# Key tiles 4 to 15 from x stored by columns: means as a row, subtraction on GpSimd, 1/std behind the products

## The chip, the cores and the metric

One Trainium2 chip, one core. The metric is the device time of one execution in microseconds; 825.71 us is the median of three runs of the kernel before (825.45 to 825.81). The engines are PE (matrix products; PEld is its weight load), DVE (vector), ACT (scalar: functions with scale and bias), POOL (GpSimd) and SP, whose queue issues the DMAs. Each engine takes its instructions in order; they wait for each other through semaphores.

## The reference

2048 tokens of width 512 go through a layer norm without weights; a linear attention block (32 heads of 16) and a mixture of 8 experts with the best 2 taken per token both read the normed tokens, and both results are added to x:

```python
phi = lambda t: jnp.where(t > 0, t + 1, jnp.exp(t)) + 1e-6
pq, pk = phi(q), phi(k)
kv = jnp.einsum("bhsd,bhse->bhde", pk, v)
z = jnp.einsum("bhsd->bhd", pk)
num = jnp.einsum("bhqd,bhde->bhqe", pq, kv)
den = jnp.einsum("bhqd,bhd->bhq", pq, z)[..., None] + 1e-6
o = num / den
...
logits = xf @ w_gate
topk_idx = jnp.argsort(-logits, axis=-1)[:, :K]
...
xn = _layernorm(x, axis=-1)
return x + _A_ref(xn, A_wqkv, A_wo) + _B_ref(xn, B_w_gate, B_w1, B_w2)
```

## The kernel before, in words

The tokens lie in 16 tiles of 128 (`NT`). Products run in fp32r: each factor is split into a high part (a copy on ACT to fp32r, line 143) and a low part (DVE: the value less the high part, line 146), and three products (high-high, high-low, low-high: `PASSES`) stand for one.

The program opens with constants, a chain of small products that keep PE busy while the first loads arrive (`keep_warm`, line 214), and tiles 0 to 2 written out by hand. Then a loop runs over t = 3 to 15, and its code order is the order of every engine's queue. In step t:

- `k_proj(t)` (line 384): 24 products of the normed tile, transposed (`xnT`, high and low), with the key weights and the gate's: 12 of 256 columns and 12 of 264 (the last 8 are the gate's logits). The third product is the first that reads a low part.
- `transp_pe(t + 1)`: four transpositions on PE that put the next tile's normed tokens by columns into PSUM. Tiles from 5 on are first copied by DMA into an fp32r tile (`xr`, line 314) so that the transposition runs in fp32r (line 329); tiles up to 4 go in fp32 (line 331). `transp_split` takes xnT's high and low parts from PSUM.
- `k_feat(t)`: phi of the keys. ACT takes the exponential of each half (line 369), DVE the minimum with 1 and the added 1e-6 (line 371) and the maximum with 0 plus that (line 375, one operand in PSUM) and copies the logits out (line 404). GpSimd adds pk to z (`z_add`, line 411, on the tile `zz`).
- `xnhl` and `pkhl`: high and low parts of the normed tile and of pk.
- `g_acc(t - 1)` (line 437): 12 products of 512 columns that sum xn' pk of the tile before into four PSUM banks.
- Layer norm ahead of time, two tiles at once: DVE takes mean and variance (`ln_stat`, lines 273 and 274), GpSimd the power -0.5 (`ln_pow`, lines 280 and 281), DVE one Newton step in four small operations (`ln_fin`, lines 286 to 290), ACT the normed tile (`ln_out`, line 305), which DMA also stores in DRAM for the experts.
- In steps 5 to 10 one half of a weight matrix is split (`split_mat`, 1024 columns: wq0l to wo1l); in steps 12 to 14 DVE does the first of the routing (`piece`, lines 496 to 528).

PSUM holds four banks for the sums, two of tag `mm` for projections and two of tag `tr` for transpositions. `constants_b`, some 30 small GpSimd operations that the routing needs later, stands after step 2 in GpSimd's queue. After the loop come the first query projection (line 1386), the last `g_acc`, z, the product with the value weights, and then the queries and experts.

Of the kernel before, what the change touches and what calls it, by code (L numbers as in the profile page):

```python
# [86 lines left out]
def linear_attn_plus_moe(  # L87
# [8 lines left out]
    wkg: bass.AP,  # L96
    out: bass.AP,
# [7 lines left out]
    ps = ctx.enter_context(tc.tile_pool(name="ps", bufs=1, space=PSUM))  # L105
# [103 lines left out]
    L = cst.tile([P, NT, E], F32, name="L")  # L209

    def keep_warm(name, n, w=P):
        warm = psm("mm", name, w)
        for i in range(n):
            T.matmul(warm, ones_b, ones_b[:, :w], start=True, stop=True)

    def constants_a():
        V.memset(ones_b, 1.0)
        G.memset(eps_t, -0.5)
        idt = raw(um("idt"))[:, :P]
        make_identity(nc, idt)  # L220
        V.tensor_copy(ident_r, idt)
        keep_warm("warm", 102, 56)

    def constants_b():
# [4 lines left out]
        G.memset(eps6, 1e-6)  # L229
# [30 lines left out]
    xnT = [sm(f"xnT{t}").rearrange("p (h k c) -> p h k c", h=2, k=KC) for t in range(NT)]  # L260
# [6 lines left out]
    lnst = {}  # L267

    def ln_stat(g, i, t):
        if i == 0:  # L270
# [4 lines left out]

    def ln_pow(g, n):
        mv = lnst[g]
        sm = wp.tile([P, 4, 2], F32, tag="sm", name=f"sm{g}", bufs=4)
        va, r0, t0, nb = (sm[:, j, :n] for j in range(4))
        (V if g == 0 else G).tensor_scalar(va, mv[:, :n, 1], EPS, None, op0=ALU.add)  # L280
        G.tensor_tensor(r0, va, eps_t[:, :n], op=ALU.pow)
        lnst[g] = (mv, va, r0, t0, nb)

    def ln_fin(g, n):
        mv, va, r0, t0, nb = lnst[g]
        V.scalar_tensor_tensor(t0, r0, -0.5, r0, op0=ALU.mult, op1=ALU.mult)
        V.tensor_tensor(t0, t0, va, op=ALU.mult)
        V.scalar_tensor_tensor(r0, t0, 1.5, r0, op0=ALU.add, op1=ALU.mult)
        if g:
            V.scalar_tensor_tensor(nb, mv[:, :n, 0], -1.0, r0, op0=ALU.mult, op1=ALU.mult)  # L290

    def ln_fin_g(g, n):
        mv, va, r0, t0, nb = lnst[g]
# [4 lines left out]
        G.tensor_tensor(r0, r0, t0, op=ALU.mult)  # L298
        G.tensor_tensor(nb, nb, r0, op=ALU.mult)

    def ln_out(g, i, t, eng):
        mv, va, r0, t0, nb = lnst[g]
        xn[t] = ta(f"xn{t}")
        if eng is A:
            A.activation(xn[t], xt[t], AF.Identity, bias=nb[:, i:i + 1], scale=r0[:, i:i + 1])
        else:
            n = 1 if t else 2
            for c in range(n):
                o = slice(c * D // n, (c + 1) * D // n)
                V.tensor_scalar(xn[t][:, o], xt[t][:, o], mv[:, i, 0:1], r0[:, i:i + 1],  # L310
                                op0=ALU.subtract, op1=ALU.mult)
# [6 lines left out]
    xr = {}  # L318
# [5 lines left out]
    def transp_pe(t):  # L324
        xtp[t] = p = psm("tr", f"xtp{t}")
        for kc in range(KC):
            o = p[:, kc * P:(kc + 1) * P]
            if t in xr:
                T.transpose(o.bitcast(F32R), xr[t][:, kc * P:(kc + 1) * P], ident_r)
            else:  # L330
                T.transpose(o, xn[t][:, kc * P:(kc + 1) * P], ident)
# [31 lines left out]

    def phi(pq, srcs, name):
        e = ta(f"e_{name}")
        o = 0
# [4 lines left out]
        V.tensor_scalar(e, e, 1.0, 1e-6, op0=ALU.min, op1=ALU.add)
        o = 0
        for src in srcs:
            w = src.shape[-1]
# [26 lines left out]
    def k_feat(t, k1, k2):  # L401
        pk = ta(f"pk{t}")
        phi(pk, (k1, k2[:, :256]), f"k{t}")
        V.tensor_copy(L[:, t, :], k2[:, 256:264])  # L404
# [5 lines left out]
    def z_add(t):  # L410
        G.tensor_tensor(zacc, zacc if t > 1 else pks.pop(0), pks.pop(t), op=ALU.add)  # L411
# [6 lines left out]
    def two_lo(hl, src):
        split_lo(hl[:, 0], hl[:, 1], src)

    def two(name, src):
        hl = tb(name).rearrange("p (h c) -> p h c", h=2)
        split(hl[:, 0], hl[:, 1], src)
# [328 lines left out]
    pk = k_feat(0, k1, k2)  # L752
# [34 lines left out]
    ln_out(4, 1, 5, A)
    constants_b()
    load_x(8)
    load_x(9)  # L790

    for t in range(3, NT):
        ks = k_proj(t)
        if t < NT - 1:
# [13 lines left out]
        pkhl = two(f"pkhl{t}", pk)  # L808
# [583 lines left out]
    def q_exp(t):  # L1392
        qp = eq[t]
        e = ta(f"e_q{t}")
        A.activation(e, qp, AF.Relu, scale=-1.0)  # L1395
        A.activation(e, e, AF.Exp, scale=-1.0)
        A.activation(e, e, AF.Identity, bias=eps6)
# [397 lines left out]
```

## Time and profile before

| | |
|---|---|
| runs, median | 825.71 us |
| the profiled execution, its own time | 827.02 us |
| its span, first to last instruction | 825.3 us |
| granted PE clock | 1.000 |
| busy: PE, DVE, ACT, POOL | 99%, 82%, 65%, 30% |
| DMA, mean over the span | 155 GB/s |

The key loop lies between 24 and 102 us of the span. The view of stages, for six pieces of two steps each (columns: busy microseconds and instructions of PE, PEld, DVE, ACT and POOL, granted clock, DMA share, GB/s):

```profile
30.00:42.00 12.00, 12.00 (x82) 11.00 (x81) 8.56 (x24) 6.56 (x14) 4.34 (x5) 1.00 0.84 291
42.00:54.00 12.00, 12.00 (x82) 10.97 (x81) 10.62 (x25) 8.15 (x15) 4.62 (x5) 1.00 0.66 215
54.00:66.00 12.00, 12.00 (x82) 10.97 (x81) 10.62 (x25) 8.14 (x15) 4.62 (x5) 1.00 0.54 190
66.00:78.00 12.00, 12.00 (x82) 10.97 (x81) 10.61 (x25) 8.13 (x15) 4.61 (x5) 1.00 0.23 88
78.00:90.00 12.00, 12.00 (x82) 10.97 (x81) 9.65 (x28) 6.18 (x13) 4.09 (x5) 1.00 0.24 89
90.00:102.00 12.00, 12.00 (x79) 10.77 (x77) 10.90 (x39) 3.67 (x9) 1.86 (x2) 1.00 0.01 1
```

PE is busy throughout; DVE has about a tenth left in the middle pieces, POOL more than half.

How to read rows: a row of the timeline gives start, length, engine, line, operation, what it writes and reads, its shape, how many equal ones are merged, and in brackets the idle time before it and what ended it. A row of the groups gives busy time and the mean of one in ns. PE's products overlap, so their pace is read from their starts.

### The profile page before, as it was taken

The page shows a single profiled execution, that of the slowest core. Times are in us where ns is not written, and L with a number is a line of the kernel's source. Part 1 is how long each engine was busy: PE and PEld are TensorE (multiplying, and loading weights), DVE is VectorE, ACT ScalarE, POOL GpSimd, SP SyncE. Part 2 cuts the span into 40 slices and gives each one's busy share as a digit, 9 for nine tenths or more (in the row PEclk, how much of TensorE's full clock was granted, in tenths as well). Part 3 has the DMA queues.
Part 4 walks back from the last instruction along what each step waited for, and adds up shares of the span by engine and source line. Part 5 has one row for each costly group of instructions (what it writes and reads, how often), then busy time and mean ns, then how long its engine had stood idle before and what let it go on. Part 6 is the DMA issues. An engine that isn't in the chain of part 4 may idle for free. (4 is left out here: it accounts for less than half of the span.)

```text
span 825.3 us, 15895 instructions
## 1 busy us (share of the span) xinstructions
PE 819.3 (99%) x5361; PEld 748.5 (91%) x5361; DVE 679.8 (82%) x1469; ACT 540.2 (65%) x1155; POOL 250.7 (30%) x344
## 2 busy tenths in 40 slices
PE   9999999999999999999999999999999999999998
PEld 8999888888899999999999999999999998888886
DVE  7788889999989868877887888788888888887852
ACT  5575464358767666766776777677768777776750
POOL 5543234376310600042604340451227023311012
PEclk9999999999999999999999999999999999999999
DMA  4752136455865853474648465746566564549507
GB/s 167 237 204 98 52 122 209 132 179 195 242 204 149 174 167 108 144 174 145 136 140 225 121 130 157 202 108 163 160 179 140 152 176 108 111 134 231 149 3 176
DMA packets 106266, 127.96 MB, mean 155 GB/s; under 512 B 14718, under 2 KB 68734, under 8 KB 106150
## 3 DMA queue, kind: packets, MB, share of 16 engines
q1 hardware_dynamic: 92294, 106.69, 43.2%
q0 software_dynamic: 12880, 18.66, 11.9%
q10 hardware_dynamic: 1008, 1.57, 0.6%
q8 instruction: 43, 0.70, 0.4%
q14 instruction: 41, 0.34, 0.1%
HBM read 94.08 MB, written 31.22 MB: 152 GB/s over the span
## 5 line engine op out<-in xcount | busy, mean ns | idle before, releaser
L1183 POOL DMA_INDIRECT out_dram<-yo,sidx x22 | 35.1, 1595 | 278.8 <-DVE yo L1178 256.4
L1183 POOL DMA_INDIRECT out_dram<-yu,L x47 | 76.6, 1630 | 92.4 <-ACT yu L1276 60.8
L146 DVE TENSOR_TENSOR h<-hs,h 128x512 fp32r<-128x512 f32 (+7 forms) x112 | 78.5, 701 | 5.5 <-ACT h L143 5.1
L143 ACT ACTIVATE h<-hs 128x512 fp32r<-128x512 f32 (+7 forms) x112 | 72.3, 646 | 3.2
L1334 ACT ACTIVATE hs<-px 128x288 f32<-128x288 f32 (+7 forms) x54 | 21.1, 390 | 54.4 <-PE px L1326 52.7
L1349 ACT ACTIVATE hs<-hs 128x288 f32<-128x288 f32 (+7 forms) x54 | 23.0, 427 | 46.6 <-DVE hs L1348 44.9
L1353 DVE TENSOR_TENSOR hs<-px,hs 128x288 f32<-128x288 f32 (+7 forms) x54 | 23.4, 433 | 34.1 <-PE px L1326 33.3
L1348 DVE TENSOR_TENSOR hs<-pz,hs 128x288 f32<-128x288 f32 (+7 forms) x54 | 23.3, 431 | 32.7 <-PE pz L1326 30.3
L437 PE MATMUL gacc<-pkhl,xnhl 128*128 128x512 f32 x192 | 47.9, 397 | 0.0
L1050 POOL DMA_INDIRECT xg<-xn_d,gidx x37 | 41.1, 1111 | 20.3 <-issue 7.2
L437 PEld LDWEIGHTS gacc<-pkhl,xnhl 128*128 128x128 f32 x192 | 34.8, 188 | 6.8
L1182 POOL MEMSET spacer<- 1x1 f32 x69 | 37.8, 547 | 7.2 <-issue 7.2
L1354 ACT ACTIVATE hs<-hs 128x288 f32<-128x288 f32 (+7 forms) x54 | 22.8, 423 | 18.0 <-DVE hs L1353 16.2
L1359 DVE TENSOR_TENSOR hs<-py,hs 128x288 f32<-128x288 f32 (+7 forms) x54 | 23.0, 425 | 13.5 <-PE py L1326 12.8
L1426 POOL TENSOR_TENSOR pz<-pq,den 128x512 f32<-128x512 f32 x16 | 17.3, 1083 | 53.0 <-DVE den L1425 51.9
L411 POOL TENSOR_TENSOR zz<-zz,pk 128x512 f32<-128x512 f32 x14 | 18.2, 1296 | 48.2 <-DVE L L404 48.2
L1395 ACT ACTIVATE e_q<-qp 128x512 f32<-128x512 f32 x16 | 9.5, 597 | 35.3 <-PE qp L1386 31.6
L1207 PE MATMUL y<-w_5h,h 128*128 128x512 f32 (+2 forms) x88 | 32.0, 394 | 0.0
L1207 PE MATMUL y<-w_1h,h 128*128 128x512 f32 (+2 forms) x88 | 32.0, 393 | 0.0
L1207 PE MATMUL y<-w_2h,h 128*128 128x512 f32 (+2 forms) x88 | 32.0, 393 | 0.0
L1207 PE MATMUL y<-w_3h,h 128*128 128x512 f32 (+2 forms) x88 | 32.0, 393 | 0.0
L1207 PE MATMUL y<-w_4h,h 128*128 128x512 f32 (+2 forms) x88 | 31.7, 393 | 0.0
(676 smaller groups left out, 3161.3 us busy)
## 6 DMA issues: line engine op xcount, KB each, us to landing
wst<-in_B_w_dram SPq DMA_DIRECT2D x196, 128.0 KB
wst<-in_B_w_dram SPq DMA_DIRECT2D x36, 512.0 KB
zz<-in_B_w_dram SPq DMA_DIRECT2D x27, 512.0 KB
xs_d<-xg SPq DMA_DIRECT2D x119, 64.0 KB
xq<-xs_d SPq DMA_DIRECT2D x28, 256.0 KB
x<-in_A_x_dram SPq DMA_DIRECT2D x27, 256.0 KB
xn_d<-xn SPq DMA_DIRECT2D x16, 256.0 KB
xnT<-xn SPq DMA_DIRECT2D x11, 256.0 KB
```

Of the source, the lines that this page charges most:

```text
L143: A.activation(hi, src, AF.Copy)
L146: V.tensor_tensor(lo, src, raw(hi), op=ALU.subtract)
L437: T.matmul(gacc[d], xnhl[:, a, d * P:(d + 1) * P], pkhl[:, b, :], start=(t == 0 and i == 0), stop=(t == NT - 1 and i == 2))
L1050: G.indirect_dma_start(out=raw(t), out_offset=None, in_=xn_d, in_offset=IOA(ap=gidx[:, b:b + 1], axis=0))
L1182: G.memset(spacer, 0.0)
L1183: st = G.indirect_dma_start(out=rows, out_offset=IOA(ap=idx, axis=0), in_=src, in_offset=None, compute_op=ALU.add).ins
L1207: T.matmul(ya[r, d][:m], h[a][:, d * P:d * P + m], w[b][:, n % 2, :], start=(first and i == 0), stop=(last and i == 2))
L1348: V.tensor_tensor(c12, pz_, c12, op=ALU.add)
L1349: A.activation(c12, c12, AF.Silu)
L1353: V.tensor_tensor(c22, px, c22, op=ALU.add)
L1354: A.activation(c22, c22, AF.Silu)
L1359: V.tensor_tensor(c11, pz_, c11, op=ALU.add)
```

## The change

For tiles 4 to 15 the key projection no longer gets its transposed operand from PE. A second input, `xcols`, holds the same x by columns, two tiles in each row of blocks; SP loads 512 KB for a pair (`load_cols`). The means of a pair, one per token and so one per partition, are brought along the row: one transposition on PE for each tile of its column of means, repeated 128 times (`means_pe`), then a copy to half of `zz` (`means`, ACT). GpSimd subtracts them from the columns (`centre`), ACT and DVE split the result into xnT's parts (`cols_hi`, `cols_lo`). The factor 1/std is left out of xnT and comes in behind the products: as the scale of the exponential and Relu for keys, as a factor of the logits, and for the queries in `q_exp` and `q_norm` through `std`, `rneg` and `estd`.

With it, phi of the keys is written as min(Relu + 1, exp), with both halves in one ACT instruction from a PSUM tile of two banks, and the 1e-6 goes into pk's split and once into z; the copies to fp32r and the 44 fp32r transpositions go; x is loaded by pairs and earlier; PSUM is divided anew (`kk`: two tiles of two banks, which transpositions, rows of means and projections share; the query's pool opens when this one closes); the warm-up has 140 products of 39 columns for 102 of 56.

```diff
-    ps = ctx.enter_context(tc.tile_pool(name="ps", bufs=1, space=PSUM))
+    ps_a = ctx.enter_context(tc.tile_pool(name="ps_a", bufs=1, space=PSUM))
+    ps_k = ExitStack()
+    ps = [ps_k.enter_context(tc.tile_pool(name="ps_k", bufs=1, space=PSUM))]
...
+    def psk(name):
+        t = ps[0].tile([P, 2 * 512], F32, tag="kk", name=name, bufs=2)
+        return t.rearrange("p (a b) -> p a b", a=2)
...
+        G.memset(eps6, 1e-6)
...
-        keep_warm("warm", 102, 56)
+        keep_warm("warm", 140, 39)
...
-        G.memset(eps6, 1e-6)
...
+        G.memset(rneg[:, :TS], -1.0)
+        G.memset(std[:, :TS], 1.0)
+        G.memset(estd[:, :TS], 1e-6)
...
+    def scales():
+        V.reciprocal(std[:, TS:], rs[:, TS:])
+        G.tensor_scalar(rneg[:, TS:], rs[:, TS:], -1.0, None, op0=ALU.mult)
+        G.tensor_scalar(estd[:, TS:], std[:, TS:], 1e-6, None, op0=ALU.mult)
...
-        if t in COPIED:
-            xr[t] = xnT[t][:, 0].rearrange("p k c -> p (k c)")
-            Q.dma_start(raw(xr[t]), xn[t])
...
+    def load_cols(g):
+        xraw[g] = wp.tile([P, SW], F32, tag="s", name=f"xraw{g}", bufs=18)
+        Q.dma_start(xraw[g], xcols[g // 2])
...
+    def means_pe(g):
+        p = mrow[g] = psk(f"mrow{g}")[:, 0, :2 * P]
+        for i in range(2):
+            T.transpose(p[:, i * P:(i + 1) * P], lnst_mv[g][:, i, 0:1].broadcast_to([P, P]), ident)
+
+    def means(g):
+        A.activation(mslot(g), mrow.pop(g), AF.Copy)
+
+    def centre(t):
+        g, i = t & ~1, t % 2
+        src = xraw[g][:, i * D:(i + 1) * D]
+        xc[t] = ta(f"xc{t}") if t == NT - 1 else src
+        if i:
+            del xraw[g]
+        src, dst = (ap.rearrange("p (k c) -> p k c", k=KC) for ap in (src, xc[t]))
+        m = mslot(g).rearrange("p (i c) -> p i c", i=2)[:, i].unsqueeze(1).broadcast_to([P, KC, P])
+        G.tensor_tensor(dst, src, m, op=ALU.subtract)
...
+    def k_feat(t, k):
+        pk, r = ta(f"pk{t}"), ta(f"r{t}")
+        sc = rs[:, t:t + 1] if t >= TS else 1.0
+        for dst, fn in ((pk, AF.Exp), (r, AF.Relu)):
+            A.activation(dst.rearrange("p (a b) -> p a b", a=2), k[:, :, :256], fn, scale=sc)
+        V.scalar_tensor_tensor(pk, r, 1.0, pk, op0=ALU.add, op1=ALU.min)
+        if t >= TS:
+            V.tensor_scalar(L[:, t, :], k[:, 1, 256:264], sc, None, op0=ALU.mult)
...
+        if t == 6:
+            G.tensor_scalar(zacc, zacc, (NT - 1) * 1e-6, None, op0=ALU.add)
...
     for t in range(3, NT):
         ks = k_proj(t)
-        if t < NT - 1:
+        if t % 2 == 0 and t + 3 < NT:
+            means_pe(t + 2)
+        nxt = t + 1 if TS <= t + 1 < NT else None
+        if t + 1 < TS:
             transp_pe(t + 1)
-        xnhl = two(f"xnhl{t}", xn[t])
+        xnhl = two_hi(f"xnhl{t}", xn[t])
+        if nxt:
+            if t % 2:
+                centre(nxt)
+            cols_hi(nxt)
+        two_lo(xnhl, xn[t])
+        if nxt:
+            cols_lo(nxt)
         if t % 2 == 0 and t + 3 < NT:
             ln_fin(t + 2, 2)
+            if t + 4 == NT:
+                scales()
...
-        pk = k_feat(t, *ks)
+        pk = k_feat(t, ks)
+        if t % 2 == 0 and t + 3 < NT:
+            means(t + 2)
+        if nxt and t % 2 and nxt + 1 < NT:
+            centre(nxt + 1)
...
-        A.activation(e, qp, AF.Relu, scale=-1.0)
+        A.activation(e, qp, AF.Relu, scale=rneg[:, t:t + 1])
         A.activation(e, e, AF.Exp, scale=-1.0)
-        A.activation(e, e, AF.Identity, bias=eps6)
+        A.activation(e, e, AF.Identity, bias=estd[:, t:t + 1], scale=std[:, t:t + 1])
```

Three places show what stands in the queues. First GpSimd's queue behind `constants_b`, whose last instruction writes `lower`; before, z's sums (L411) and the next pair's power (L280, L281) follow it:

```order
L255 AFFINE_SELECT lower_113<-ones_r_97 128x64
L411 TENSOR_TENSOR zz_114<-zz_114,pk3_616 128x512
L280 TENSOR_SCALAR sm6_633<-mv6_535 128x2
L281 TENSOR_TENSOR sm6_633<-sm6_633,eps_t_98 128x2
L411 TENSOR_TENSOR zz_114<-zz_114,pk4_689 128x512
```

and now, with the subtractions (L384, on the columns `xraw`):

```order
L275 AFFINE_SELECT lower_115<-ones_r_100 128x64
L384 TENSOR_TENSOR xraw4_492<-xraw4_492,zz_116 128x512
L470 TENSOR_TENSOR zz_116<-zz_116,pk3_647 128x512
L384 TENSOR_TENSOR xraw4_492<-xraw4_492,zz_116 128x512
L301 TENSOR_SCALAR sm6_661<-mv6_566 128x2
L302 TENSOR_TENSOR sm6_661<-sm6_661,eps_t_101 128x2
L470 TENSOR_TENSOR zz_116<-zz_116,pk4_719 128x512
```

Tile 4's subtraction is the first thing behind the constants, and the power for tiles 6 and 7 stands behind tile 5's, which stands behind z's sum of pk(3).

Second, ACT's queue in step 9. Before, the exponentials of the two halves (L369) stand ahead of the next tile's xnT:

```order
L143 ACTIVATE xnhl9_1079<-xn9_866 128x512
L369 ACTIVATE e_k9_1083<-k1_9_1048 128x256
L369 ACTIVATE e_k9_1083<-k2_9_1049 128x256
L143 ACTIVATE xnT10_127<-xtp10_1074 128x512
L143 ACTIVATE pkhl9_1096<-pk9_1082 128x512
```

and now xnT of tile 10, from the subtracted columns, stands ahead of the exponential and Relu (L458):

```order
L150 ACTIVATE xnhl9_1079<-xn9_885 128x512
L150 ACTIVATE xnT10_1082<-xraw10_880 128x512
L458 ACTIVATE pk9_1086<-k_9_1054,rs_119 128x512
L458 ACTIVATE r9_1087<-k_9_1054,rs_119 128x512
L477 ACTIVATE pkhl9_1097<-pk9_1086,eps_t_101 128x512
```

Third, DVE's queue from the end of step 8 to pk's low part of step 9. Before:

```order
L146 TENSOR_TENSOR pkhl8_1021<-pk8_1002,pkhl8_1021 128x512
L146 TENSOR_TENSOR wv1l_1029<-wvst1_842,wv1h_1028 128x1024
L146 TENSOR_TENSOR xnhl9_1079<-xn9_866,xnhl9_1079 128x512
L371 TENSOR_SCALAR e_k9_1083<-e_k9_1083 128x512
L375 SCALAR_TENSOR_TENSOR pk9_1082<-k1_9_1048,e_k9_1083 128x256
L375 SCALAR_TENSOR_TENSOR pk9_1082<-k2_9_1049,e_k9_1083 128x256
L404 COPY L_116<-k2_9_1049 128x8
L146 TENSOR_TENSOR xnT10_127<-xtp10_1074,xnT10_127 128x512
L273 BN_STATS bs13_1093<-x13_888 128x6
L274 BN_AGGR mv12_1017<-bs13_1093 128x2
L146 TENSOR_TENSOR pkhl9_1096<-pk9_1082,pkhl9_1096 128x512
```

and now:

```order
L484 SCALAR_TENSOR_TENSOR pkhl8_1032<-pk8_1015,pkhl8_1032 128x512
L153 TENSOR_TENSOR wv1l_1039<-wvst1_862,wv1h_1038 128x1024
L153 TENSOR_TENSOR xnhl9_1079<-xn9_885,xnhl9_1079 128x512
L153 TENSOR_TENSOR xnT10_1082<-xraw10_880,xnT10_1082 128x512
L459 SCALAR_TENSOR_TENSOR pk9_1086<-r9_1087,pk9_1086 128x512
L461 TENSOR_SCALAR L_118<-k_9_1054,rs_119 128x8
L293 BN_STATS bs13_1094<-x12_822 128x6
L294 BN_AGGR mv12_1026<-bs13_1094 128x2
L484 SCALAR_TENSOR_TENSOR pkhl9_1097<-pk9_1086,pkhl9_1097 128x512
```

xnT's low part has moved ahead of pk and reads SBUF (`xraw`) for PSUM (`xtp`); pk is one operation of two SBUF tiles for three operations, two of which read PSUM (k1, k2).

More of the change, by code (lines that the diff above doesn't have):

```diff
@@ L209, in linear_attn_plus_moe @@
     L = cst.tile([P, NT, E], F32, name="L")
+    rs = cst.tile([P, NT], F32, name="rs")
+    rneg = cst.tile([P, NT], F32, name="rneg")
+    std = cst.tile([P, NT], F32, name="std")
+    estd = cst.tile([P, NT], F32, name="estd")
     def keep_warm(name, n, w=P):
-        warm = psm("mm", name, w)
+        warm = psk(name)[:, 0, :w]
         for i in range(n):
@@ L217, in constants_a @@
         V.memset(ones_b, 1.0)
-        G.memset(eps_t, -0.5)
+        G.memset(eps_t[:, :2], -0.5)
+        G.memset(eps6, 1e-6)
         idt = raw(um("idt"))[:, :P]
@@ L257, in constants_b @@
                         channel_multiplier=0)
-    xnT = [sm(f"xnT{t}").rearrange("p (h k c) -> p h k c", h=2, k=KC) for t in range(NT)]
+    xnT = {}
     def xT(t, hl, kc):
@@ L411, in z_add, with two_hi, two_lo, two @@
         G.tensor_tensor(zacc, zacc if t > 1 else pks.pop(0), pks.pop(t), op=ALU.add)
-    def two_hi(name, src):
+        if t == 6:
+            G.tensor_scalar(zacc, zacc, (NT - 1) * 1e-6, None, op0=ALU.add)
+    def two_hi(name, src, eps=False):
         hl = tb(name).rearrange("p (h c) -> p h c", h=2)
-        split_hi(hl[:, 0], src)
-        return hl
[L418 to L423, printed above, removed]
+        if eps:
+            A.activation(hl[:, 0], src, AF.Identity, bias=eps6)
+        else:
+            split_hi(hl[:, 0], src)
+        return hl
+    def two_lo(hl, src, eps=False):
+        if eps:
+            V.scalar_tensor_tensor(hl[:, 1], src, 1e-6, raw(hl[:, 0]), op0=ALU.add, op1=ALU.subtract)
+        else:
+            split_lo(hl[:, 0], hl[:, 1], src)
+    def two(name, src, eps=False):
+        hl = two_hi(name, src, eps)
+        two_lo(hl, src, eps)
         return hl
@@ L807, in linear_attn_plus_moe @@
             ln_stat((t + 4) & ~1, t % 2, t + 4)
-        pkhl = two(f"pkhl{t}", pk)
+            if t % 2 == 0:
+                load_cols(t + 4)
+        pkhl = two(f"pkhl{t}", pk, True)
         if t % 2 == 1 and t + 4 < NT:
@@ L818, in linear_attn_plus_moe @@
             piece(1 + (t == NE + 2))
-        if t % 2 == 0 and t + 7 < NT:
-            load_x(t + 6)
+        if t % 2 and t + 8 < NT - 1:
+            load_x2(t + 7)
+        elif t % 2 and t + 8 == NT - 1:
             load_x(t + 7)
+            load_x(t + 8)
+    ps_k.close()
+    ps[0] = ctx.enter_context(tc.tile_pool(name="ps_q", bufs=1, space=PSUM))
     M_v = []
@@ L1423, in q_norm @@
         den = dens.pop(t)
-        V.tensor_scalar(den, den, 1e-6, None, op0=ALU.add)
+        V.tensor_scalar(den, den, estd[:, t:t + 1], None, op0=ALU.add)
         V.reciprocal(den, den)
```

139 lines of the change are left out of this document (76 added, 63 removed).

## The prediction

> **What bounds the kernel now.** I read the page's first part, then the list of who waited for whom on PE, then PE's instructions in order of time.
>
> ```profile
> span 825.3 us, 15895 instructions
> PE 819.3 (99%) x5361; PEld 748.5 (91%) x5361; DVE 679.8 (82%) x1469; ACT 540.2 (65%) x1155; POOL 250.7 (30%) x344
> PE warm L214 <- DVE ones_b L217: 1.1, 1, 1.1
> ...
> PE xtp L331 <- ACT xn L305: 0.3, 1, 0.3
> 24.30 0.28 PE L384 MATMUL k<-wk1h,xnT 128*128 128x256 f32 x1
> 27.18 0.60 PE L331 MATMUL xtp<-ident_r,xn 128*128 128x128 f32 x4
> 27.54 3.00 PE L437 MATMUL gacc<-pkhl,xnhl 128*128 128x512 f32 x12
> 30.37 0.28 PE L384 MATMUL k<-wk1h,xnT 128*128 128x256 f32 x1
> 33.25 0.45 PE L329 MATMUL xtp<-ident_r,xnT 128*128 128x128 f32 x4
> 33.54 2.97 PE L437 MATMUL gacc<-pkhl,xnhl 128*128 128x512 f32 x12
> 36.35 0.28 PE L384 MATMUL k<-wk1h,xnT 128*128 128x256 f32 x1
> 96.42 0.28 PE L384 MATMUL k<-wk1h,xnT 128*128 128x256 f32 x1
> 102.29 0.50 PE L1386 MATMUL qp<-wq0h,xnT 128*128 128x512 f32 x1
> ```
>
> PE is busy in 99% of the span, and the four waits of its list (first and last shown) are short. So only PE's own row can be shortened, and whatever makes PE wait is paid in full. In the key loop the first column gives the pace: 24 projection products take 27.18 - 24.30 = 2.88 us, 12 products of the sum 30.37 - 27.54 = 2.83 us, four transpositions 33.54 - 33.25 = 0.29 us. One key tile lasts 36.35 - 30.37 = 5.98 us.
>
> **PE's own work.** Eleven tiles lose four transpositions at 0.29 us, tile 4 loses four of the fp32 kind at 27.54 - 27.18 = 0.36: 3.55 us gone. Six pairs get two single fp32 transpositions for the means, 0.36/4 = 0.09 each: 1.08 us (0.9 to 1.4, with 0.29/4 and a projection product's 0.12 as ends). Net **-2.5 us**. A key tile then takes 5.71 us on PE, 5.89 with a row of means: 11.6 us a pair.
>
> **The warm-up**, 102 products of 56 columns, becomes 140 of 39.
>
> ```profile
> 1.15 4.91 PE L214 MATMUL warm<-ones_b 128*128 128x56 bf16 x102 [1.15 <-DVE ones_b L217]
> 6.57 0.76 PE L359 MATMUL xtp<-ident_r,xn 128*128 128x128 f32 x4 [0.51 <-DVE xn L310]
> ```
>
> One starts every (4.91 - 0.23)/101 = 46 ns. If that is the price of an instruction, 140 end at 7.6 us and the first transposition, at 6.57 now, is 1.1 us late; if it is the columns' price, they end at 5.7 us and cost nothing. I take 0, since the total of columns is nearly the old one, and keep +1.1 for the range. The Trainium skill (TensorE: Matmul & The Clock Gate, "Wait — 56ns, not 53.3ns?") gives a start-to-start of N ÷ 1.2 GHz in a cold array, 46.7 ns for 56 columns; the measured 46 agrees, and by that rule the answer is 0.
>
> **A wait at tile 4.** Its columns need GpSimd's subtraction, and in POOL's queue that stands behind all of `constants_b`.
>
> ```profile
> 24.35 0.10 POOL L229 MEMSET eps<- 128x1 f32 x1
> 24.39 0.29 POOL L230 CAST ones_r<-ones_b 128x128 fp32r<-128x128 bf16 x1
> ...
> 28.94 0.30 POOL L255 TENSOR_SCALAR_AFFINE_SELECT lower<-ones_r 128x64 f32<-128x64 f32 x1
> 29.45 1.30 POOL L411 TENSOR_TENSOR zz<-zz,pk 128x512 f32<-128x512 f32 x1 [0.21 <-DVE L L404]
> L143 ACT ACTIVATE xnT<-xtp 128x512 fp32r<-128x512 f32 x15 | 8.9, 594 | 0.9 <-PE xtp L331 0.9
> L1426 POOL TENSOR_TENSOR pz<-pq,den 128x512 f32<-128x512 f32 x16 | 17.3, 1083 | 53.0 <-DVE den L1425 51.9
> ```
>
> The constants end at 28.94 + 0.30 = 29.24; one memset moves out, three small ones come (0.04 from start to start): about 29.4. The subtraction has no row; the nearest is GpSimd's sum of the same size, 1.30 (1.08 with the broadcast of L1426 is the other end). It ends at 30.7, ACT's high part (0.6) at 31.4, DVE's low part (0.68) at 32.1. PE would want tile 4 at 24.30 + 0.18 + 2.88 + 2.83 = 30.2, and its third product, the first with a low part, at 30.4. It gets it at 32.1: **+1.7 us** (+1.4 with 1.08). Behind the waiting `xnT4` on ACT stand the exponentials of tile 3, so all the evacuation that follows is late too.
>
> **The port between DVE and GpSimd.** This decides the rest.
>
> ```profile
> 30.77 0.66 DVE L146 TENSOR_TENSOR pkhl<-pk,pkhl 128x512 fp32r<-128x512 f32 x1
> 83.81 1.23 DVE L146 TENSOR_TENSOR pkhl<-pk,pkhl 128x512 fp32r<-128x512 f32 x1
> 83.19 1.30 POOL L411 TENSOR_TENSOR zz<-zz,pk 128x512 f32<-128x512 f32 x1 [2.85 <-DVE L L404]
> 187.69 2.39 DVE L146 TENSOR_TENSOR w_0l<-wst,w_0h 128x512 fp32r<-128x512 f32 x2
> 187.85 1.68 POOL L1407 TENSOR_TENSOR pz<-pq,zz 128x512 f32<-128x512 f32 x1 [0.55 <-DVE pq L1403]
> 53.07 0.68 DVE L146 TENSOR_TENSOR xnT<-xtp,xnT 128x512 fp32r<-128x512 f32 x1
> 53.22 1.30 POOL L411 TENSOR_TENSOR zz<-zz,pk 128x512 f32<-128x512 f32 x1 [4.77 <-DVE L L404]
> ```
>
> The low part of pk takes 0.66 us alone. Started under GpSimd's sum, it ends 0.55 after it (83.81 + 1.23 = 85.04 against 83.19 + 1.30 = 84.49): it stood still until GpSimd was through. At 187.69 two DVE instructions and one of GpSimd run strictly in turn: 0.55 + 1.29 + 0.55 = 2.39. The xnT row at 53.07, one operand from PSUM, is not slowed. Now the change moves work into this collision: xnT's low part reads xraw in SBUF instead of PSUM, pk comes from two SBUF tiles, and GpSimd gets a second large operation per tile. The Trainium skill (SBUF — State Buffer, "Who interferes with whom") says that a DVE instruction with two SBUF inputs contends with a GpSimd one that reads SBUF, and that the one issued later fully blocks. These rows agree; by that rule the new pk operation, which no row shows, waits as well, and the sum is the one below; were pk free, it would drop by little, since pk stands where GpSimd is idle.
>
> By the order of the queues a closed chain now runs from pk(t) to pk(t+1): GpSimd adds pk(t) to z, then subtracts a tile's means; ACT takes that tile's high part, and behind it in ACT's queue stand the exponential and Relu of t+1; DVE makes pk(t+1) from these. In between DVE's queue holds pk's, the weights', xnhl's and xnT's low parts, all with two SBUF inputs.
>
> ```profile
> 55.06 1.22 DVE L146 TENSOR_TENSOR wv0l<-wvst,wv0h 128x1024 fp32r<-128x1024 f32 x1
> 56.19 0.68 DVE L146 TENSOR_TENSOR xnhl<-xn,xnhl 128x512 fp32r<-128x512 f32 x1
> 55.30 1.54 POOL L281 TENSOR_TENSOR sm<-sm,eps_t 128x2 f32<-128x2 f32 x1
> 56.88 0.16 DVE L286 SCALAR_TENSOR_TENSOR sm<-sm 128x2 f32<-128x2 f32 x1
> 57.46 0.16 DVE L290 SCALAR_TENSOR_TENSOR sm<-mv,sm 128x2 f32<-128x2 f32 x1
> L1397 ACT ACTIVATE e_q<-e_q,eps 128x512 f32<-128x512 f32 x6 | 4.3, 724 | 0.2
> L1396 ACT ACTIVATE e_q<-e_q 128x512 f32<-128x512 f32 x6 | 3.8, 632 | 0.2
> L1395 ACT ACTIVATE e_q<-qp 128x512 f32<-128x512 f32 x6 | 3.6, 600 | 8.8 <-PE qp L1386 8.8
> 91.03 0.24 DVE L496 TENSOR_REDUCE arena<-arena 128x12 f32<-128x96 f32 x1
> 92.94 0.68 DVE L146 TENSOR_TENSOR xnhl<-xn,xnhl 128x512 fp32r<-128x512 f32 x1
> 97.03 0.16 DVE L516 TENSOR_SCALAR arena<-arena 128x12 f32<-128x12 f32 x1
> 100.75 0.69 DVE L146 TENSOR_TENSOR xnhl<-xn,xnhl 128x512 fp32r<-128x512 f32 x1
> ```
>
> - From an even tile, with a weight to split (8, 10): sum 1.35, pk low 0.55, subtraction 1.30, weight low 1.10 (start to start, 55.06 to 56.19), xnhl low 0.60, xnT low 0.60, pk 0.66: **6.15**. Tile 6 has a scaling of z on top (0.9; between 0.3 and 1.3): 7.1. Tile 4 has no weight; there ACT's path of 1.95 follows the subtraction: xnT high 0.65, exponential 0.60, Relu 0.70 (0.60 from PSUM by L1395; 0.1 more where the pipeline drains, for an operand from a tile, as L1397 against L1396): 3.2 + 1.95 + 0.66 = 5.8.
> - From an odd tile: GpSimd's power for the next pair now stands behind the subtraction, and DVE's four small Newton operations (56.88 to 57.62, 0.75) wait for it and stand ahead of pk: 5, 7, 9 take 3.2 + 1.1 + 0.2 + 0.55 + 0.6 + 0.75 + 0.66 = **7.05**; 3, without a weight, 6.6; 11, which also has no wait for the power left, 6.2.
> - A row of means takes one of the two projection buffers in PSUM, so product t + 1 waits for ACT's copy of it (0.4) behind Relu(t); in these sums that copy ends before pk(t) and adds nothing.
> - 12 and 13 have no weight but the routing's steps ahead of xnhl (92.94 - 91.03 = 1.9, part of it under GpSimd): 6.6 each.
>
> A pair with weights takes 13.2 us against PE's 11.6, so PE waits. Steps 3 to 13 add up to 6.6 + 5.8 + 7.05 + 7.1 + 7.05 + 6.15 + 7.05 + 6.15 + 6.2 + 6.6 + 6.6 = 72.4 us. pk(3) ends at 33.3 (xnT4 high begun at 30.75, then 0.6 for it, 0.6 and 0.7 for exponential and Relu, 0.66 for pk), so pk(14) at 105.7. Tile 15's third projection product, freed by the xnT low part just ahead of pk(14), comes at 105.1; it stands at 96.42 + 0.24 = 96.66 now: **+8.4 us**, in which PE's saving and tile 4's wait are contained.
>
> After that the first query product takes memory that tile 15's evacuation frees; behind pk(14) come 1.35 + 0.55, the routing's 100.75 - 97.03 = 3.7, xnhl 0.60, pk(15) 0.66 and the logits 0.15: 7.0, so 112.7 against 102.29: **+10.4 us**. From there on PE never waited for long and DVE, ACT and GpSimd do nearly the old work, so I pass it on whole; a scale or bias from a tile instead of a constant in the query features lies beside PE's rows. DMA changes from eleven copies of 256 KB to six loads of 512 KB, issued a pair ahead; I cost it at 0.
>
> 825.3 + 10.4 is a span of 835.7. The profiled execution itself took 827.02, 1.31 over the median 825.71 of the runs, so I take the same difference on the median: 836.0.
>
> **Rivals.** That the change doesn't do what it says is out: PE's order has no transposition of x behind tile 3.
> - *Half a chain.* If DVE's low parts slip between GpSimd's two operations better than I let them, only the port's own sum counts: 4 x 1.30 + 8 x 0.55 + 2 x 1.10 and 0.3 for small ones, 12.1 against 11.6 in three pairs: +1.5, with 1.7 and -2.5 some +0.7; anything up to +7 lies between. Against it: z's sum waits for pk(t), so GpSimd has nothing to do earlier. 827 to 833.
> - *Not slower.* The one mechanism is that the subtraction and the new DVE operations run side by side. Then the chain is 1.35 + 1.30 + 0.65 + 0.60 + 0.70 + 0.70 = 5.3 from an even tile and 1.35 + 1.30 + 0.45 + 1.3 + 0.75 + 0.70 = 5.9 from an odd one, 11.2 a pair: under PE's 11.6, the point from which it decides. What is left is -2.5 + 1.7 and some 0.5 behind tile 4: **825.4**. For it: no row has these very operations; against it: every 128x512 pair that met did block.
> - *Faster.* The same, and tile 4 is not late: 825.7 - 2.5 = 823.2. It needs the constants to end 1.7 us sooner; POOL's rows speak against it.
> - *Warm-up by the instruction*: +1.1 on any of them, 837.1.
>
> **How the numbers follow.** Forecast with its warm-up variant 0.66, half a chain 0.14, not slower 0.10, faster 0.08, beyond it all 0.02. The forecast's own range is 833 (subtraction at 1.08: 11 x 0.22 less, scaling 0.3) to 838.5 (warm-up, scaling 1.3, weight at 1.22). With the half chain this holds 0.8, so the range is 826.5 to 838.5. About 0.2% can be told from no change here: slower 0.79, within 0.13, faster 0.08.
>
> **What would show it.** PE waiting for xnT about 1.7 us at the fourth key tile and about 0.7 to 1 us in most later ones; DVE's low parts in the key loop at 1.2 or more in their means; GpSimd's subtraction at 1.3 or longer; the first query product at about 112. I am wrong if DVE's rows stay at 0.68 beside a busy GpSimd, if the subtraction of tile 4 starts before 29, or if PE shows no wait behind tile 5.

## The result, and the profile after

| | before | after |
|---|---|---|
| runs, median | 825.76 us (825.45 to 826.36, 4 runs) | 837.65 us (836.11 to 838.53, 4 runs) |
| ratio of the runs, 95% interval | | 1.0141 [1.0124, 1.0159] |
| span of the profiled execution | 825.3 us | 835.6 us |
| first query product begins | 102.29 us | 111.02 us |

The change costs 1.4%. The page of the changed kernel, first part, and then its list of who waited for whom on PE (microseconds in all, times, the longest):

```profile
span 835.6 us, 15855 instructions
PE 822.1 (98%) x5363; PEld 746.1 (89%) x5363; DVE 687.5 (82%) x1440; ACT 553.7 (66%) x1161; POOL 277.0 (33%) x362
```

```profile
PE k L427 <- DVE xnT L153: 2.7, 6, 0.8
PE qp L1478 <- DVE L L461: 2.1, 1, 2.1
PE k L427 <- ACT xnT L150: 1.8, 2, 0.9
...
PE k L427 <- ACT zz L374: 1.1, 3, 0.5
```

PE's busy time rose by 2.8 us although it has less to do, and three new waits stand where before there was none: for xnT's two parts, for the copy of the rows of means, and one of 2.1 us ahead of the first query product. PE's instructions of the changed kernel in order of time show where the 10.3 us of span arise:

```profile
30.79 0.38 PE L427 MATMUL k<-wk1h,xnT 128*128 128x256 f32 x1 [0.89 <-ACT xnT L150]
...
31.52 0.51 PE L427 MATMUL k<-wk1h,xnT 128*128 128x256 f32 x2 [0.22 <-DVE xnT L153]
...
103.27 0.51 PE L427 MATMUL k<-wk1h,xnT 128*128 128x256 f32 x2 [0.62 <-DVE xnT L153]
...
111.02 0.47 PE L1478 MATMUL qp<-wq0h,xnT 128*128 128x512 f32 x1 [2.09 <-DVE L L461]
...
118.20 0.39 PE L1478 MATMUL qp<-wq0h,xnT 128*128 128x512 f32 x1
```

Tile 15's third product is 103.27 - 96.66 = 6.6 us late, the first query product 111.02 - 102.29 = 8.7. The second query projection begins at 118.20, where it began at 107.86 before: 10.3. So 6.6 us come from the key loop, 2.1 from the wait behind it, and 1.6 from something between the first and the second query projection. The waits of PE's list in the loop come to only 5.6 us, and PE should have saved some there. PE's weight loads (PEld) tell the rest: between 20 and 125 us they wait 3.9 and 2.6 us for xnT's two parts, 3.2 for the copies of the rows of means and 1.8 for pk's low part, 11.5 us in all, where the kernel before has none of these. For the 1.6 us, the view of stages from 109 to 118 us (columns as in the table of six pieces) says what happens:

```profile
109.00:112.00 3.00, 0.98 (x4) 0.86 (x5) 2.27 (x7) 0.73 (x1) 1.12 (x1) 1.00 0.00 0
112.00:115.00 3.00, 3.00 (x9) 2.38 (x8) 2.66 (x12) 0.00 (x0) 0.63 (x2) 0.57 0.51 190
115.00:118.00 3.00, 3.00 (x13) 2.38 (x12) 0.67 (x5) 2.57 (x5) 0.00 (x0) 0.86 0.67 250
```

Behind the wait PE's granted clock, the number behind POOL's column, falls to 0.57 and 0.86: PE is busy throughout, but at little over half its pace, and 0.43 x 3 + 0.14 x 3 = 1.7 us are lost.

The port: GpSimd's and DVE's instructions of the changed kernel in order of time.

```profile
28.52 0.29 POOL L275 TENSOR_SCALAR_AFFINE_SELECT lower<-ones_r 128x64 f32<-128x64 f32 x1
28.80 1.28 POOL L384 TENSOR_TENSOR xraw<-xraw,zz 128x512 f32<-128x512 f32 x1
...
33.76 1.74 POOL L384 TENSOR_TENSOR xraw<-xraw,zz 128x512 f32<-128x512 f32 x1
...
52.75 1.83 POOL L472 TENSOR_SCALAR zz<-zz 128x512 f32<-128x512 f32 x1
```

```profile
31.74 0.69 DVE L459 SCALAR_TENSOR_TENSOR pk<-r,pk 128x512 f32<-128x512 f32 x1 [0.28 <-ACT r L458]
...
34.28 1.77 DVE L153 TENSOR_TENSOR xnhl<-xn,xnhl 128x512 fp32r<-128x512 f32 x1
...
46.42 2.31 DVE L153 TENSOR_TENSOR wq0l<-wqst,wq0h 128x1024 fp32r<-128x1024 f32 x1
...
103.13 0.68 DVE L459 SCALAR_TENSOR_TENSOR pk<-r,pk 128x512 f32<-128x512 f32 x1
...
110.05 0.68 DVE L459 SCALAR_TENSOR_TENSOR pk<-r,pk 128x512 f32<-128x512 f32 x1
```

The subtraction takes 1.28 us where DVE is idle (28.80) and 1.74 beside DVE's low parts; xnhl's low part, 0.68 alone, takes 1.77 beside it and ends 0.55 behind it (36.05 against 35.50); a weight's, 1.22 before, takes up to 2.31. The new pk operation runs where GpSimd is idle and keeps 0.69; the rows shown are those of tiles 3, 14 and 15.

### The profile page after: what moved, and what is told of

Read it like the earlier page. It is cut to its first block, busy times and chain, and to the rows that moved or that the text cites. A ratio compares the mean times of both kernels' runs of the same rounds, so it can differ in the third digit from the quotient of the medians.

```text
span 835.6 us, 15855 instructions
## 1 busy us (share of the span) xinstructions
PE 822.1 (98%) x5363; PEld 746.1 (89%) x5363; DVE 687.5 (82%) x1440; ACT 553.7 (66%) x1161; POOL 277.0 (33%) x362
## 5 line engine op out<-in xcount | busy, mean ns | idle before, releaser
L150 ACT ACTIVATE h<-hs 128x512 fp32r<-128x512 f32 (+7 forms) x112 | 72.4, 646 | 3.2
L1426 ACT ACTIVATE hs<-px 128x288 f32<-128x288 f32 (+7 forms) x54 | 21.1, 391 | 56.7 <-PE px L1418 56.6
L1487 ACT ACTIVATE e_q<-qp,rneg 128x512 f32<-128x512 f32 x16 | 11.0, 688 | 36.0 <-PE qp L1478 29.2
L1436 ACT ACTIVATE hs<-px 128x288 f32<-128x288 f32 (+7 forms) x54 | 21.2, 392 | 16.4 <-PE px L1418 15.1
```

The lines of the kernel that those rows point to most:

```text
L150: A.activation(hi, src, AF.Copy)
```

## The experiments

The theory: DVE's operations with two operands in SBUF stand still while GpSimd's new subtraction reads SBUF; by the order of the queues a closed chain from pk(t) over GpSimd and ACT to pk(t+1) sets the pace. Rivals: the port alone without the chain; DVE simply too full; GpSimd's queue, whatever it reads; the shared PSUM buffers. Ratios are to the kernel before on the same chip, with their 95% intervals.

**1. The chain cut.** All work stays; the sum for z comes one step later, so that no subtraction stands behind a sum that needs the newest pk.

```diff
-        if t > 2:
-            z_add(t)
+        if t > 3:
+            z_add(t - 1)
...
+    z_add(NT - 1)
     ps_k.close()
```

> GpSimd adds pk to z one step later, so that no subtraction stands behind a sum that waits for the newest pk. All work stays. Theory (closed chain through GpSimd's queue, on top of the shared port): the wait of the subtraction for pk(t) goes, what is left is the port's own sum, about 12.1 us a pair against 12.76 measured between pk(8) and pk(10); some 0.6 us in five to six pairs, 834 us (832 to 836). Rival A (the port alone: DVE loses the same time wherever GpSimd's two operations stand): within 1 us of 837.65. Rival B (only the queue's chain, the port is nothing): the first query product at 103 to 104, 828 us or less.

Measured: 837.76 us (836.9 to 839.15), 1.0144 [1.0127, 1.0161], the first query product at 111.85. Rival A held. Was the chain really cut? The list of ACT's waits between 30 and 112 us, of the changed kernel and then of this one:

```profile
ACT xnT L150 <- POOL xraw L384: 13.6, 9, 2.9
```

```profile
ACT xnT L150 <- POOL xraw L384: 4.0, 2, 2.9
```

It was: ACT's nine waits for GpSimd's subtraction became two. What DVE then did instead is in the groups of DVE's instructions in the loop (count | busy us, mean ns), again of the changed kernel and then of this one:

```profile
L484 DVE SCALAR_TENSOR_TENSOR pkhl<-pk,pkhl 128x512 fp32r<-128x512 f32 x11 | 12.1, 1104 | 1.3 <-ACT pkhl L477 1.3
L153 DVE TENSOR_TENSOR xnhl<-xn,xnhl 128x512 fp32r<-128x512 f32 x11 | 11.6, 1055 | 0.2 <-ACT xnhl L150 0.2
L153 DVE TENSOR_TENSOR xnT<-xraw,xnT 128x512 fp32r<-128x512 f32 x11 | 7.5, 686 | 3.4 <-ACT xnT L150 3.1
```

```profile
L153 DVE TENSOR_TENSOR xnhl<-xn,xnhl 128x512 fp32r<-128x512 f32 x10 | 11.9, 1191 | 0.4 <-ACT xnhl L150 0.4
L153 DVE TENSOR_TENSOR xnT<-xraw,xnT 128x512 fp32r<-128x512 f32 x11 | 11.2, 1017 | 2.8 <-ACT xnT L150 2.8
L484 DVE SCALAR_TENSOR_TENSOR pkhl<-pk,pkhl 128x512 fp32r<-128x512 f32 x11 | 9.7, 885 | 1.4 <-ACT pkhl L477 1.4
```

Against 0.66 to 0.68 alone these three stand still for 11 x 0.44 + 11 x 0.38 = 9.0 us in the changed kernel, and for 10 x 0.51 + 11 x 0.34 + 11 x 0.22 = 11.3 here. The weights' low parts gain (4.0 us of standstill become 0.9), small operations lose; with all of DVE's rows from pk(3) to pk(14), each one's time less what it takes alone, it is 14.7 us in the changed kernel and 16.4 here, and about 1.8 in as many steps of the kernel before. The subtraction, no longer held back, only meets other operations of DVE, and the steps from pk(3) to pk(14) take 71.6 us (33.08 to 104.64) where they took 71.4. So the chain is not what costs: without it the standstill is no less. One thing blurs this: PE's clock fell at tile 4 in this execution (see the last section), and DVE waited 0.70 us for Relu there, so up to 0.7 us of gain may be hidden.

**2. The subtraction on DVE**, at the same places in the program.

```diff
-        G.tensor_tensor(dst, src, m, op=ALU.subtract)
+        V.tensor_tensor(dst, src, m, op=ALU.subtract)
```

> The subtraction runs on DVE at the same places in the program. DVE gets 12 more operations of about 0.6 us from start to start (1.2 us a pair), GpSimd keeps the sum for z. Theory (chain and port): of 12.76 us a pair about 1.7 of blocking and 0.6 of waiting go, so the pair comes to 11.7 to 11.9, near PE's own 11.6; the wait for GpSimd's constants at tile 4 goes too. 829 us (827 to 831.5), xnhl's and the weights' low parts back at 0.68 and 1.22 except under the sum for z. Rival (DVE is simply full, each operation more costs): 12 x 0.6 = 7 us on top, 840 or more.

Measured: 832.22 us (831.0 to 832.29), 1.0067 [1.005, 1.0083]; the first query product at 105.00, 6.0 us sooner. DVE got twelve operations more and the kernel became 0.7% faster (the ratio was 1.0141), so DVE is not simply full. Two things go at once here: pk(3) starts at 29.30 where it started at 31.74, since nothing at tile 4 waits for GpSimd's constants any more, and that is 2.4 of the 6.0 us; the other 3.6 arise between pk(3) and pk(15). The groups of DVE:

```profile
L484 DVE SCALAR_TENSOR_TENSOR pkhl<-pk,pkhl 128x512 fp32r<-128x512 f32 x12 | 13.0, 1080 | 1.4 <-ACT pkhl L477 1.3
...
L153 DVE TENSOR_TENSOR xnhl<-xn,xnhl 128x512 fp32r<-128x512 f32 x11 | 7.5, 681 | 0.0
```

xnhl is back at 0.68; pkhl still meets the sum for z. The time is 0.7 us above the range expected: the wait ahead of the first query product stayed at 2.1 us, and the clock fell behind it here too (0.55 in 106 to 109 us).

**3. Without the subtraction** for tiles 4 to 14.

```diff
-        G.tensor_tensor(dst, src, m, op=ALU.subtract)
+        if t == NT - 1:
+            G.tensor_tensor(dst, src, m, op=ALU.subtract)
```

> Leaves out the subtraction of the means for tiles 4 to 14 (tile 15 keeps it); rows of means and their copies stay. Theory: without GpSimd's second operation neither chain nor most of the blocking is left, PE goes at its own pace and shows its saving of 2.5 us but for a first-query wait of 1 to 2 us: 825 us (823 to 828). Rival (the two shared PSUM buffers of the projections, or ACT's order, hold PE up, not the subtraction): 833 or more.

Measured: 826.03 us (825.06 to 827.5), 0.9998 [0.9988, 1.0008]; PE busy without a gap from 30 to 90 us, first query product at 100.26 behind a wait of 1.7. The subtraction, with its late start, is the whole cost: the PSUM buffers and ACT's order hold nothing up. And even at no price for it the change as written is no gain, since the wait behind the loop stays.

**4. The port alone**: the kernel before, with one more GpSimd operation for each key tile.

```diff
         if t > 2:
             z_add(t)
+            G.tensor_tensor(zb, xn[t], xn[t], op=ALU.subtract)
```

> The kernel before, with one more GpSimd operation for each key tile from 3 on, behind the sum for z: xn less xn, 128x512, into the unused half of zz. Nobody waits for its result. Theory (port): DVE's low parts of xnhl and of the weights wait for it, 0.5 to 1.2 us each; DVE has 1.4 us free in 12, so a pair of tiles comes to 12.3 to 13 us instead of 12: 829 us (827 to 832), and DVE rows of 1.2 us and more that were 0.68. Rival (GpSimd's work beside DVE costs nothing unless something waits for it): 825.8 within 0.8.

Measured: 831.4 us (830.93 to 831.87), 1.0062 [1.0045, 1.0079]. Nobody reads the result, and it costs 5 us. GpSimd's rows and then DVE's:

```profile
54.72 1.55 POOL L408 TENSOR_TENSOR zz<-xn 128x512 f32<-128x512 f32 x1
```

```profile
55.29 2.06 DVE L146 TENSOR_TENSOR wv0l<-wvst,wv0h 128x1024 fp32r<-128x1024 f32 x1
```

The weight's low part, 1.22 without it, ends 1.08 behind the dummy (57.35 against 56.27): nearly its whole length comes after the dummy's end.

**5. GpSimd busy without reading**: the same place, but an iota (it only writes); one for each tile (without the loop of the diff), and then three, since one took 0.56 us and left the length open.

```diff
         if t > 2:
             z_add(t)
+            for _ in range(3):
+                G.iota(zb, pattern=[[1, D]], base=0, channel_multiplier=0,
+                       allow_small_or_imprecise_dtypes=True)
```

> The kernel before, with one more GpSimd operation for each key tile from 3 on at the same place as the dummy subtraction, but one that reads nothing: an iota of 512 columns into the unused half of zz, estimated at about 1.1 us from the iota of 128 columns at 0.35 and of 64 at 0.23. Theory (DVE stands still only beside a GpSimd operation that reads SBUF): DVE's low parts keep their times, 826 (825.2 to 827). Rival (any GpSimd operation beside DVE holds it up, or the longer GpSimd queue does): 829 or more, as with the subtraction that nobody reads.

> As the kernel before with the iota, but three of them for each key tile: the one iota took 0.56 us, where the dummy subtraction took 1.33 in the mean, so it left open whether the length of GpSimd's work counts; three take 1.6 to 1.7. Theory (DVE stands still only beside a GpSimd operation that reads SBUF): 826.4 within 0.8, DVE's xnhl and pkhl rows at 0.68 and 0.81 in the mean as without them. Rival (as much GpSimd time as in the dummy subtraction costs as much, whatever it reads, if only by keeping its queue late): 830 or more.

Measured: one iota 1.0002 [0.9993, 1.0012] (826.84 us against 826.44), three 1.0013 [1.0003, 1.0023] (827.2 against 826.29). With three, GpSimd's rows and then DVE's at the same place:

```profile
53.83 1.83 POOL L409 IOTA zz<- 128x512 f32 x3
```

```profile
53.90 0.66 DVE L146 TENSOR_TENSOR pkhl<-pk,pkhl 128x512 fp32r<-128x512 f32 x1
54.47 1.22 DVE L146 TENSOR_TENSOR wv0l<-wvst,wv0h 128x1024 fp32r<-128x1024 f32 x1
```

1.83 us of GpSimd beside them, longer than the dummy's 1.55, and both keep their times. GpSimd's queue is late here too: in the loop (24 to 104 us) DVE waits 5.8 us for the layer norm's power, more than the 3.3 us beside the dummy, and the kernel loses 0.1% where the dummy cost 0.6%. It is the reading that blocks, not GpSimd's being busy. The Trainium skill (SBUF — State Buffer, "Who interferes with whom") says just this, that DVE with two SBUF inputs contends with a GpSimd instruction that reads SBUF and not with one that only writes it; these rows agree.

**6. The constants early**: ahead of everything else on GpSimd instead of ahead of the first subtraction (`constants_c` is the second part of `constants_b`).

```diff
     constants_a()
+    constants_b()
     ln_stat(0, 0, 0)
...
     ln_fin_g(1, 1)
+    constants_c()
...
-    constants_b()
     load_x2(8)
```

> GpSimd's constants are made at the start (most of them in the gap from 1.5 to 4.7 us, the rest behind the layer norm of tile 1) instead of ahead of the first subtraction. The subtraction of tile 4 can then begin at 26.0 us, when its means are there, in place of 28.8, and pk(3) can end at about 29.7 in place of 32.43. Theory (from pk(3) to pk(15) DVE's row, held up by the port, has no room, so what it loses at the start is never made good): the whole 2.7 us come out at the end, 835.0 (834.3 to 836). Rival A (only PE's own wait at tile 4 counts, 1.1 us): 836.5. Rival B (the room behind takes it up): 837.65 within 0.7.

Measured: 834.7 us (833.36 to 835.52), 1.0108 [1.0093, 1.0124].

```profile
108.31 0.47 PE L1481 MATMUL qp<-wq0h,xnT 128*128 128x512 f32 x1 [2.08 <-DVE L L463]
```

111.02 - 108.31 = 2.7 us, to the tenth what was expected. PE waited only 1.1 us at tile 4, but the start of DVE's row was 2.7 late, and nothing behind it made that good. The gap of 2.08 us ahead of the query is the same as before; here the clock did not fall behind it.

**7. The gap filled**: 37 products without a reader in the 2.1 us ahead of the first query product.

```diff
+    keep_warm("warm_c", 37)
     ps_k.close()
```

> 37 products of 128 columns, whose result nobody reads, stand between the last sum of the key loop and the first query product, about the 2.1 us that PE waits there. Nothing else is changed, the wait stays. Theory (PE's clock is halved for some 3 us behind this gap, which the trace shows as 0.57 and 0.86 of full speed in 112 to 118 us, and it is the gap that does it): the clock stays at 1.00 in 106 to 120 us in every run, the query's products keep 0.23 us from start to start, 836.2 (835.8 to 836.8). Rival (the clock falls for another reason): the same fall behind the filler, 837.65.

Measured: 836.76 us (836.46 to 838.43), 1.0137 [1.0121, 1.0152]; first query product at 111.24. The view of stages behind the filler:

```profile
112.00:115.00 3.00, 3.00 (x15) 2.45 (x14) 2.66 (x12) 0.67 (x1) 0.75 (x2) 1.00 0.47 177
115.00:118.00 3.00, 3.00 (x15) 2.49 (x14) 1.51 (x10) 2.93 (x7) 0.00 (x0) 1.00 0.71 263
```

The clock stays at 1.00, and the query's products come 15 in 3 us where they came 9. The median is within the range expected, but the intervals of the two ratios (1.0141 for the changed kernel) overlap almost wholly, so the times don't show a gain. "In every run" failed: one of four still had a lower mean clock (0.998), the one of 838.43; a run gives only the mean, so where it fell stays open. And since the clock does not fall behind every such wait (experiment 6), one execution without a fall does not prove that the filler prevents it.

**8. The wait taken away**: the second half of the routing's early steps behind tile 15's evacuation.

```diff
-            piece(1 + (t == NE + 2))
+            piece()
...
+    piece()
     ps_k.close()
```

> The second half of the routing's early steps, 3.7 us of DVE between pkhl(14) and xnhl(15), comes behind tile 15's evacuation instead. Theory (the first query product waits for the logits' copy of tile 15, which stands behind these steps): that copy ends at 108.3, before PE is through with its sum at 108.9; the wait of 2.1 us and the fall of the clock behind it (1.5 us) go: 834.1 (833.5 to 835.5), first query product at about 109. Rival (the 3.7 us come back on DVE ahead of the sums' evacuation and the query features): 836.5 or more.

Measured: 835.66 us (835.52 to 836.26), 1.0118 [1.0103, 1.0134]: 0.2 us above the range. The first query product went at 109.28 without a wait, and the clock stayed up, but the list of PE's waits has a new line:

```profile
PE pos_ps L620 <- DVE arena L615: 1.0, 1, 1.0
```

The steps are now late for the product that counts the tokens of each expert: PE waits 1.0 us there, and 0.3 for the next result of DVE.

**9. Together**: the subtraction on DVE, the even tile's ahead of the weight's low part of the step before, and the routing steps as in 8.

```diff
-            if t % 2:
+            if t == 3:
                 centre(nxt)
...
         pkhl = two(f"pkhl{t}", pk, True)
+        if t % 2 == 0 and t + 2 < NT:
+            centre(t + 2)
```

> The subtraction on DVE, that of the even tile ahead of the weight's low part of the step before instead of behind it, and the routing steps behind tile 15's evacuation. Theory (with the port free of the subtraction and no wait at the first query product PE sets the pace and shows its 2.5 us): first query product at 99.5 to 100.5 us, 823.5 (822.5 to 825). Rival (DVE's row of 11.7 to 11.9 us a pair stays longer than PE's 11.6 and the waits only move): 827 to 829.

Measured: 825.46 us (824.89 to 826.91), 0.9996 [0.9987, 1.0005]: no difference that can be told, and above the range. PE's instructions:

```profile
32.72 0.38 PE L371 MATMUL mrow<-ident_r,mv 128*128 128x128 f32 x2
32.85 2.97 PE L504 MATMUL gacc<-pkhl,xnhl 128*128 128x512 f32 x12
...
44.18 0.38 PE L371 MATMUL mrow<-ident_r,mv 128*128 128x128 f32 x2
...
98.42 0.39 PE L1481 MATMUL qp<-wq0h,xnT 128*128 128x512 f32 x1
...
107.77 0.22 PE L620 MATMUL pos_ps<-arena,ones_b 128*128 128x136 bf16 x1 [1.03 <-DVE arena L615]
```

Here PE does go at its own pace: a pair takes 44.18 - 32.72 = 11.46 us, a row of means 0.13, and the first query product begins 3.9 us sooner than before the change. Of these 0.2 lie ahead of the loop: from its first product it takes 98.42 - 24.12 = 74.3 us where the kernel before took 102.29 - 24.30 = 78.0, so the loop itself is 3.7 shorter. (When the loop starts differs by up to 1 us between executions; in the kernel with one iota it began at 23.63 and took the same 78.0.) But 1.0 of it goes in the wait for the routing and 0.3 in the next one, and the query tiles lose some 0.6 more.

**10. And the counts on GpSimd**: routing back at its old place, its twelve running counts of 8 columns on GpSimd.

```diff
+            e = G if ts.start == 0 else V
...
-                V.tensor_tensor(inc[:, t + 1, :], inc[:, t, :], mask[:, t, :], op=ALU.add)
+                e.tensor_tensor(inc[:, t + 1, :], inc[:, t, :], mask[:, t, :], op=ALU.add)
```

> As the kernel with the subtraction on DVE and that of the even tile moved ahead, the routing's steps back at their old place, and its twelve running counts of 8 columns (2.38 us on DVE) on GpSimd, which has nothing to do there. Theory (of the 3.9 us that PE gains up to the first query product, 1.4 are lost because DVE's routing steps are late for the next PE group): first query product near 98.4 us, no wait of PE for the routing's result at 107, the second query projection 3.5 to 3.9 us ahead of the kernel before; with 0.65 us lost over the query tiles 824.0 (823.4 to 824.8). Rival (the gain is taken back by whatever is next, or GpSimd's twelve operations hold DVE up through the port): 825.4 as the one before it.

Measured: 824.54 us (823.39 to 825.31), 0.9973 [0.9963, 0.9984] to 826.44 on that chip. This version beats both kernels: it is 0.27% under the one before and, by the two ratios (0.9973/1.0141), 1.7% under the changed one.

```profile
107.61 0.23 PE L621 MATMUL pos_ps<-arena,ones_b 128*128 128x136 bf16 x1
```

No wait is left there. In the profiled run the first query product stands at 99.44, with a wait of 1.06 us for a key weight's low part at 12.5 us ahead of it, at the start; without that it is the 98.4 expected.

## Why the prediction held, and where its steps did not

- **PE's own work** was mis-sized. Forecast -2.5 us; with nothing in its way the loop came out 3.7 shorter (experiment 9). The row of means costs 0.13 a pair and not 0.18, and a pair takes 11.46 us and not 11.6; and a tile before, read at 5.98, takes (96.42 - 30.37)/11 = 6.00 in the mean.
- **The warm-up** cost nothing, as forecast: 140 products of 39 columns took 4.85 us, (4.85 - 0.23)/139 = 33 ns each against 46 for 56 columns, so columns are what is paid. That rival is out.
- **The wait at tile 4**: forecast 1.7, measured 0.89 + 0.22 = 1.1, because the constants ended at 28.81 and not 29.4. So the subtraction began at 28.80, and one of the prediction's own signs of being wrong, a start before 29, came true; it stood for a term 0.6 too large, not for a wrong mechanism. That the start carries through to the end was right, and experiment 6 prices it at 2.7.
- **The port** was right, in size too: in the loop xnhl's low part goes from 0.68 to 1.06 in the mean and pk's from 0.81 to 1.10 (a little under the 1.2 named as a sign), a weight's from 1.22 to as much as 2.31, and "not slower" and "faster" fall with it. Shown by 2 in the changed kernel, by 4 and 5 in the kernel before. The steps from pk(3) to pk(14) were forecast at 72.4 and took 71.4 (31.74 + 0.69 = 32.43 to 103.13 + 0.68 = 103.81). One term was far off: the scaling of z took 1.83, not 0.9, outside its bounds of 0.3 to 1.3; and the step from 11, "which also has no wait for the power left", took 6.6 and not 6.2, with a wait of DVE for that power of 0.60 us. The copy of a row of means, said to add nothing, made PE wait three times, 1.1 us in all.
- **The closed chain** is the step that failed as a cause: "By the order of the queues a closed chain now runs from pk(t) to pk(t+1)". It gives the right dates, since each link waits for the one before; but cut (experiment 1) it saves nothing. In its place stands DVE's row: its own work, the time that it stands still (14.7 us, and 16.4 where GpSimd's two operations fall otherwise) and short waits for ACT and GpSimd; it is busy 63.6 of the 72 us from 30 to 102, and 64.5 with the chain cut. What the chain would cost if the standstill had stayed the same is not shown. "Half a chain", which counted on less, is out too.
- **The first query product** waits for tile 15's evacuation, as said: 2.09 us, behind 110.05 - 103.13 = 6.9 of DVE's row (7.0 forecast). It came at 111.02 and not 112.7, by the smaller sums above.
- **"I pass it on whole"** failed. The clock fell behind that wait and added 1.6 us, which the forecast did not have. So the span of 835.6 against 835.7 is luck, two errors that cancel: 1.7 too much up to the query, 1.6 too little behind it. For the runs they do not cancel: 836.0 was forecast, on the assumption that the profiled execution lies 1.31 us above the median as it did before, and the median is 837.65, 0.39 above the profiled one. The one run of the four whose mean clock was 1.000 took 836.11; the others, at 0.998, 837.26 to 838.53.

## What to carry to other kernels

An idle GpSimd is not free room beside a DVE that is 90% busy: where a GpSimd operation that reads SBUF met DVE operations with two operands there, each of these lost up to 1.1 us (0.68 to 1.77, 1.22 to 2.31), and another place in GpSimd's queue only moved the loss; here twelve subtractions on GpSimd cost more than twelve on DVE itself, even without their late start. When a chain of waits explains every date, cut one link before you believe it: the dates may be those of one engine whose row is full. And where a stage has been paced by PE, shortening PE moves the bound to the next row that is nearly full (here the routing's small steps on DVE), so most of 3.9 us was to be had only when these were moved as well.

## What was not expected of the hardware

Behind 1.5 to 2.1 us of idle PE the granted clock was halved for some 3 us, but not each time. It fell in the changed kernel behind 2.09 us (0.57 and 0.86 in 112 to 118 us), in experiment 2 behind 2.10, and in experiment 1 at tile 4, where PE was idle for 1.5 us of three in two waits, 0.90 and 0.62 (view of stages):

```profile
30.00:33.00 3.00, 1.49 (x8) 0.85 (x7) 1.61 (x2) 1.60 (x3) 1.92 (x2) 0.97 1.02 385
33.00:36.00 3.00, 3.00 (x16) 3.00 (x16) 2.95 (x8) 1.76 (x3) 1.86 (x3) 0.50 1.04 401
```

In all thirteen profiled executions, read in steps of one microsecond up to 820 us, it fell below 0.98 in these three places only. It did not fall behind 2.09 us at the first query product of experiment 1, 2.08 in 6, 1.71 in 3 and 1.62 in 4. The Trainium skill (TensorE: Matmul & The Clock Gate, "Part 1: The HAM clock gate") tells of a window of about 3.4 us that runs freely and of a clock that is either whole or half. The 0.50 over three whole microseconds and the dependence on chance agree; that it takes an idle window of that length does not, since it fell behind 1.5 to 2.1 us here.

GpSimd's own operation is held up in turn: 1.28 us where DVE is idle, 1.74 beside DVE's low parts. So both sides of the port pay.
